# Recording VectorE and ScalarE in program order, with attention and norms placed by a clock at emission

## The chip, the cores and the metric

One core of a Trainium2 chip. The metric is device time in microseconds (us) of one execution; lower is better. Executions of one kernel in one set of runs lie within about 0.25% of each other (the kernel before beside the experiments, 27 runs: 1635.41 to 1638.25 us). The profiled span of a kernel is 1 to 2 us shorter than its timed median.

## The reference

Two rounds of a local attention layer and a gated feed-forward, each with a residual, on 2048 tokens of width 1024 in bf16 (F = 3584, 32 heads, window of 8 keys at distance 2):

```python
x = x + attention(layernorm(x), wqkv, wo)    # q.k over 8 keys, softmax, weighted sum of v, then @ wo
x = x + (silu(n @ w1) * (n @ w3)) @ w2       # n = layernorm(x)
# the same two lines once more, with the same weights
```

## The kernel before

Tokens go in 4 chunks of 512. Matmuls leave their sums in banks of 512 columns; copying a bank out, so that TensorE can use it again, is called evacuation here. A chunk passes the QKV projection (`ps`), attention in two halves of 256 tokens (on VectorE: products `pr` and `tm`, each summed by a tree of adds), the output projection (`po`, called an o-tile, one for 128 tokens), a layer norm, and the feed-forward (gate `pg`, up `pu`, down `acc`). q, k and v travel through DRAM to change their layout. TensorE stands in program order; the other engines are ordered by a scheduler with priorities.

```python
    ctx.enter_context(tc.manual_schedule(engines={mybir.EngineType.PE}))
    ...
    def tree_sum8(buf, dst):
        nc.vector.tensor_tensor(buf[:, 0:4, :], buf[:, 0:4, :], buf[:, 4:8, :], op=ALU.add)
        nc.vector.tensor_tensor(buf[:, 0:2, :], buf[:, 0:2, :], buf[:, 2:4, :], op=ALU.add)
        nc.vector.tensor_tensor(dst, buf[:, 0, :], buf[:, 1, :], op=ALU.add)
    ...
    for c in range(NCH):                       # the first layer's QKV, and attention of chunk 0
        for which in range(3):
            q_part(0, c, which)
            ...                                # cut: load x of later chunks
            if which == 1 and c == 1:
                nc.sync.dma_start(wo[:], wo_v)
            ...                                # cut: norm of the next chunk, o_tile(0, 0)
            if c == 3 and which == 1:
                o_tile(0, 1)
                ln_half(("B", 0, 0), 0, 0)     # norm for the first feed-forward
                o_tile(0, 2)
                o_tile(0, 3)
                ln_half(("B", 0, 0), 0, 1)
    ...                                        # cut
    # in the feed-forward, per 128 columns of F: 8 matmuls pg, 8 matmuls pu, then
                    with hp():                 # priority over attention
                        sg = sgp.tile([P, CH], BF16, name="sg")
                        nc.scalar.activation(sg[:], pg[:], ACTF.Silu)
                        nc.vector.tensor_tensor(hT[:, g0 + fi - f0, :], sg[:], pu[:], op=ALU.mult)
```

## Time and profile before

| | before |
|---|---|
| time, median of 4 runs | 1636.94 us (1636.28 to 1638.18) |
| profiled span | 1635.4 us |
| 7424 matmuls of 512 columns at 0.2158 us | 1602.3 us |
| start of the first QKV matmul | 13.92 us |
| beyond 1602.3 us, from there to the last matmul's end | 15.50 us |
| last matmul's end to the span's end | 3.69 us |

The 0.2158 us is a start-to-start distance: 192 undisturbed matmuls take 41.44 us. (The mean of 380 ns in the profile is the latency of one matmul; matmuls overlap.) I found the 15.50 us by listing every pair of neighbouring matmul starts that lie further apart than that. The three terms of the table and the first matmul's start add up to the span: 13.92 + 1602.3 + 15.50 + 3.69 = 1635.4.

The page's busy line, of the kernel before:

```profile
PE 1616.1 (99%) x7472; PEld 800.2 (49%) x7472; DVE 1152.4 (70%) x1961; ACT 340.5 (21%) x530; POOL 1.9 (0%) x12
```

Groups of TensorE's instructions, of the kernel before; the last column is idle time ahead of the group and who ended it:

```profile
L305 PE MATMUL pg<-xnT,w1t 128*128 128x512 bf16 x1792 | 424.7, 380 | 4.9 <-DMA xnT<-xn 4.9
...
L327 PE MATMUL acc<-w2t,hT 128*128 128x512 bf16 x1792 | 390.8, 379 | 5.1 <-DVE hT L314 4.7
L202 PE MATMUL ps<-xnT,wqkv 128*128 128x512 bf16 x1536 | 334.3, 380 | 1.8 <-ACT xnT L163 1.1 <-DVE x_sb L287 0.7
L283 PE MATMUL po<-wo,oT 128*128 128x512 bf16 x512 | 115.4, 379 | 0.0
```

TensorE is nearly full. What idles does so before the first feed-forward (waiting for its transposed norm), in the down projection (for the last product hT), and a little in QKV. The o-tiles wait for nothing.

TensorE's timeline at the first feed-forward, of the kernel before (start, duration, what, in brackets the idle time and its releaser):

```profile
187.09 8.85 PE L202 MATMUL ps<-xnT,wqkv 128*128 128x512 bf16 x40 [0.66 <-DVE x_sb L287]
200.80 3.28 PE L305 MATMUL pg<-xnT,w1t 128*128 128x512 bf16 x8 [4.86 <-DMA xnT<-xn]
203.87 2.23 PE L309 MATMUL pu<-xnT,w3t 128*128 128x512 bf16 x8
```

Eight matmuls normally take 1.89 us on this view; here 3.28, because after the 5 us of idling the next eight matmuls start 0.427 us apart instead of 0.216: half pace. And at the first down projection:

```profile
257.74 3.40 PE L327 MATMUL acc<-w2t,hT 128*128 128x512 bf16 x15
263.25 7.08 PE L327 MATMUL acc<-w2t,hT 128*128 128x512 bf16 x32 [2.11 <-DVE hT L314]
```

Fifteen matmuls use the first 15 slices of hT, the 16th waits for VectorE, where a 2.3 us transpose and a 1.2 us product of attention stood ahead of the last hT (259.03 to 262.51 us). VectorE sets this because it is full in the first third of the program. Windows of the kernel before, with busy time and, in brackets, number of instructions of each engine:

```profile
40.00:200.00 160.00, 155.28 (x719) 99.86 (x717) 149.88 (x263) 52.87 (x96) 0.00 (x0) 1.00 0.63 182
200.00:352.00 152.00, 147.23 (x673) 66.16 (x674) 150.48 (x251) 28.73 (x41) 0.00 (x0) 0.99 0.55 166
352.00:505.00 153.00, 152.25 (x707) 68.86 (x705) 151.98 (x262) 31.61 (x43) 0.00 (x0) 1.00 0.54 164
```

(third column: VectorE, 149.88 of 160, 150.48 of 152, 151.98 of 153 us). Where that begins is on VectorE's timeline:

```profile
53.04 0.17 DVE L129 RECIPROCAL rstd<-sd 128x2 f32<-128x2 f32 x1 [0.42 <-ACT sd L128]
56.59 2.36 DVE L228 TENSOR_TENSOR pr<-qT,kT 128x2048 bf16<-128x2048 bf16 x2 [3.38 <-DMA kT<-qkv_d_1_159]
```

Attention starts at 56.6 us, when its first keys (`kT`) land.

### The profile page before, as it was taken

To read this page: it belongs to the slowest core of one execution; us is meant where nothing else is said; L and a number is where in the kernel's file an instruction comes from. 1 tells how busy PE (TensorE), PEld (TensorE's weight loads), DVE (VectorE), ACT (ScalarE), POOL (GpSimd) and SP (SyncE) were. 2 spreads that over 40 slices of the span, in tenths; PEclk is the share of its full clock that TensorE was granted. 3 is DMA by queue.
4 is the path that set the end of the run, shared out by engine and by line. 5 is a ranking of instruction groups with operands and counts; after the bars stand their busy time and mean duration, and the time that the engine had idled before them with its cause. 6 is when DMAs were issued, how large, how long until landed. Compare 5 with 4: busy or idle time off the path is not lost.

```text
span 1635.4 us, 18944 instructions
## 1 busy us (share of the span) xinstructions
PE 1616.1 (99%) x7472; PEld 800.2 (49%) x7472; DVE 1152.4 (70%) x1961; ACT 340.5 (21%) x530; POOL 1.9 (0%) x12
## 2 busy tenths in 40 slices
PE   8999899999999999999999999999999999999999
PEld 5666444444444644446444554445544444444444
DVE  4899999999999781897728977299652992332212
ACT  3333311203021320223202232022320211121110
POOL 0000000000000000000000000000000000000000
PEclk9999999999999999999999999999999999999999
DMA  9943746557546774367743686438753574256440
GB/s 297 280 132 102 220 158 195 159 151 209 183 131 180 240 235 150 106 193 245 221 142 104 199 259 200 142 104 249 255 178 119 129 232 155 90 143 205 155 129 26
DMA packets 337113, 286.32 MB, mean 175 GB/s; under 512 B 69632, under 2 KB 319488, under 8 KB 336896
## 3 DMA queue, kind: packets, MB, share of 16 engines
q1 hardware_dynamic: 337024, 285.11, 57.2%
q8 instruction: 58, 0.95, 0.2%
q14 instruction: 31, 0.25, 0.0%
HBM read 239.99 MB, written 29.36 MB: 165 GB/s over the span
## 4 chain that ended last, share of the span: by engine, by line
PE 67%; DVE 29%; issue 3%; DMA 1%; ACT 0%; DVEq 0%; ACTq 0%
PE acc L327 21%; PE pg L305 15%; PE pu L309 15%; PE ps L202 13%; DVE pr L228 5%; DVE tm L273 4%; PE po L283 3%; DVE hT L314 3%; DVE tm L174 3%; DVE pr L174 2%; DVE x_sb L287 1%; DVE st L124 1%; DVE tm L175 1%; DVE pr L175 1%; DVE L L235 1%
## 5 line engine op out<-in xcount | busy, mean ns | idle before, releaser
L305 PE MATMUL pg<-xnT,w1t 128*128 128x512 bf16 x1792 | 424.7, 380 | 4.9 <-DMA xnT<-xn 4.9
L309 PE MATMUL pu<-xnT,w3t 128*128 128x512 bf16 x1792 | 423.7, 379 | 0.0
L327 PE MATMUL acc<-w2t,hT 128*128 128x512 bf16 x1792 | 390.8, 379 | 5.1 <-DVE hT L314 4.7
L202 PE MATMUL ps<-xnT,wqkv 128*128 128x512 bf16 x1536 | 334.3, 380 | 1.8 <-ACT xnT L163 1.1
L313 ACT ACTIVATE sg<-pg 128x512 bf16<-128x512 f32 x224 | 133.4, 597 | 843.2 <-PE pg L305 831.4
L314 DVE TENSOR_TENSOR hT<-sg,pu 128x512 bf16<-128x512 bf16 x224 | 152.1, 679 | 212.2 <-PE pu L309 210.7
L305 PEld LDWEIGHTS <-w1t 128*128 128x128 bf16 x1792 | 175.5, 98 | 217.0 <-issue 6.6
L327 PEld LDWEIGHTS <-hT 128*128 128x128 bf16 x1792 | 174.8, 98 | 218.5 <-DVE hT L314 9.0
L309 PEld LDWEIGHTS <-w3t 128*128 128x128 bf16 x1792 | 175.5, 98 | 212.0 <-issue 1.0
L202 PEld LDWEIGHTS <-wqkv 128*128 128x128 bf16 x1536 | 220.5, 144 | 114.6 <-issue 3.9
L332 DVE TENSOR_TENSOR x_sb<-x_sb,acc 128x512 bf16<-128x512 bf16 x128 | 87.0, 680 | 162.2 <-PE acc L327 162.2
L228 DVE TENSOR_TENSOR pr<-qT,kT 128x2048 bf16<-128x2048 bf16 x128 | 153.1, 1210 | 51.6 <-issue 32.1
L273 DVE TENSOR_TENSOR tm<-At,vT 128x2048 bf16<-128x2048 bf16 x128 | 151.7, 1213 | 0.3
L204 ACT CAST sgt<-ps 128x512 bf16<-128x512 f32 x192 | 108.7, 588 | 184.6 <-PE ps L202 151.7
L283 PE MATMUL po<-wo,oT 128*128 128x512 bf16 x512 | 115.4, 379 | 0.0
L124 DVE BATCH_NORM_STATS2 st<-x_sb 128x6 f32<-128x512 bf16 x120 | 79.9, 681 | 18.0 <-DMA x_sb<-in_A_x_dram 17.3
L174 DVE TENSOR_TENSOR pr<-pr 128x1024 bf16<-128x1024 bf16 x128 | 85.6, 680 | 0.0
L174 DVE TENSOR_TENSOR tm<-tm 128x1024 bf16<-128x1024 bf16 x128 | 84.4, 681 | 0.0
L283 PEld LDWEIGHTS <-oT 128*128 128x128 bf16 x512 | 50.0, 98 | 60.4
L287 DVE TENSOR_TENSOR x_sb<-x_sb,po 128x512 bf16<-128x512 bf16 x64 | 43.2, 677 | 15.4 <-PE po L283 15.4
L175 DVE TENSOR_TENSOR pr<-pr 128x512 bf16<-128x512 bf16 x128 | 51.8, 415 | 0.2
L175 DVE TENSOR_TENSOR tm<-tm 128x512 bf16<-128x512 bf16 x128 | 50.3, 415 | 0.1
(169 smaller groups left out, 428.7 us busy)
## 6 DMA issues: line engine op xcount, KB each, us to landing
w1t<-in_B_w_dram SPq DMA_DIRECT2D x56, 1024.0 KB, 5.4
w3t<-in_B_w_dram SPq DMA_DIRECT2D x56, 1024.0 KB, 7.2
w2t<-in_B_w_dram SPq DMA_DIRECT2D x48, 1024.0 KB, 5.4
wqkv<-in_A_wqkv_dram SPq DMA_DIRECT2D x28, 1024.0 KB, 6.6
w2t<-in_B_w_dram SPq DMA_DIRECT2D x16, 512.0 KB, 5.1
qkv_d_0_158<-sgt SPq DMA_DIRECT2D x16, 256.0 KB, 5.3
qkv_d_1_159<-sgt SPq DMA_DIRECT2D x16, 256.0 KB, 4.4
qT<-qkv_d_0_158 SPq DMA_DIRECT2D x8, 512.0 KB, 4.0
```

The costliest lines, as they stand in the source:

```text
L174: nc.vector.tensor_tensor(buf[:, 0:4, :], buf[:, 0:4, :], buf[:, 4:8, :], op=ALU.add)
L175: nc.vector.tensor_tensor(buf[:, 0:2, :], buf[:, 0:2, :], buf[:, 2:4, :], op=ALU.add)
L202: nc.tensor.matmul(ps[:], lhsT=ws[kk // KH][:, kk % KH, t::KT], rhs=xnT[:, kk, :], start=(kk == 0), stop=(kk == KT - 1))
L204: nc.scalar.copy(sgt[:, t - t0, :], ps[:])
L228: nc.vector.tensor_tensor(pr[:], qT[:], kT[:, :, k0:k0 + TCH], op=ALU.mult)
L273: nc.vector.tensor_tensor(tm[:], At[:], win, op=ALU.mult)
L283: nc.tensor.matmul(ps[:], lhsT=oT[:, t, j * P:(j + 1) * P], rhs=wo[:, t, hh * 512:(hh + 1) * 512], start=(t == 0), stop=(t == KT - 1))
L305: nc.tensor.matmul(pg[:], lhsT=w1t[:, kk, fi * P:(fi + 1) * P], rhs=xnT[:, kk, :], start=(kk == 0), stop=(kk == KT - 1))
L309: nc.tensor.matmul(pu[:], lhsT=w3t[:, kk, fi * P:(fi + 1) * P], rhs=xnT[:, kk, :], start=(kk == 0), stop=(kk == KT - 1))
L313: nc.scalar.activation(sg[:], pg[:], ACTF.Silu)
L314: nc.vector.tensor_tensor(hT[:, g0 + fi - f0, :], sg[:], pu[:], op=ALU.mult)
L327: nc.tensor.matmul(acc[:], lhsT=hT[:, f - f0, j * P:(j + 1) * P], rhs=w2ts[(f - f0) // 8][:, (f - f0) % 8, :], start=(f == f0), stop=(f == ...
```

## The change

VectorE and ScalarE also go into program order. Attention and norms become Python generators of single steps, each with a cost. While the program is emitted, a small clock keeps track of where TensorE, VectorE and ScalarE should be; before each evacuation of a bank it places as many attention steps as should end in time. O-tiles are emitted as soon as the clock says that their input is ready. The aim is that no evacuation stands behind a long attention instruction. The head is reworked too: x arrives on two queues, the fourth tile's statistics move to ScalarE, warm matmuls fill TensorE's gaps.

```diff
-    ctx.enter_context(tc.manual_schedule(engines={mybir.EngineType.PE}))
+    ctx.enter_context(tc.manual_schedule(engines={mybir.EngineType.PE, mybir.EngineType.DVE,
+                                                  mybir.EngineType.Activation}))
+    MM, TABLE, DMA = 0.216, 1.3, 2.5
+    x_at = [12.5] + [20.0 + 10 * c for c in range(1, NCH)]
+    def background(until):                      # norms first, then attention
+        while True:
+            for queue in (norms, attention):
+                s = head(queue)
+                if s is not None and max(now["dve"], s[1]) + s[0] <= until:
+                    take(queue)
+                    break
+            else:
+                return
 ... cut: the clock's counters, the norms as generators, the head
+    def tree(n, mul, dst):                      # attention's sums, interleaved
+        yield 1.14, 0.0, lambda: first(0)
+        for i in range(n):
+            yield 0.605, 0.0, lambda: half(i, 4)
+            if i:
+                yield 0.21, 0.0, lambda: half(i - 1, 1)
+            if i + 1 < n:
+                yield 1.14, 0.0, lambda: first(i + 1)
+            yield 0.34, 0.0, lambda: half(i, 2)
+        yield 0.27, 0.0, lambda: half(n - 1, 1)
 ... cut
+        qks[l, h] = qT, kT, max(now["dve"], qkv_at[l, h // R, 1]) + DMA     # keys "ready"
 ... cut
+            if c == NCH - 1 and which == 2:
+                between(False, True)            # force the o-tiles of chunk 0
             q_part(0, c, which)
 ... cut: the feed-forward
+                    r = max(pe(KT), ts)
+                    background(r + slack)       # slack -0.5 for the last two hT, else 1.0
+                    nc.vector.tensor_tensor(hT[:, f - f0, :], sg[:], pu[:], op=ALU.mult)
```

## The prediction

> **What bounds it.** TensorE: the page shows it busy 1616 of 1635.4 us at a granted clock of 0.998. There are 7424 matmuls of 512 columns; in undisturbed runs of the trace 192 of them take 41.44 us, 0.2158 us each, so they need 1602.3 us in any order. VectorE (70%) and ScalarE (21%) cannot set the total, but from 40 to 505 us VectorE is busy 94 to 99% (windows by stage), and there its order matters.
>
> **What can be won.** From the starts of consecutive matmuls, all beyond 1602.3 us:
> - 13.9 us before the first QKV matmul, then about 1.35 us lost at a slow pace (0.427 us apart). That is the unwarmed pace of the Trainium skill ("TensorE: Matmul & The Clock Gate", Part 1); this trace agrees.
> - 0.9 us at 187 us (QKV waits for a bank that VectorE frees late).
> - 5.0 us at 200.8 us: the first feed-forward waits for its normalised input, whose VectorE steps stood behind attention; then 1.6 us at the slow pace.
> - 2.3, 2.0 and 0.9 us at 263, 347 and 425 us, and five times 0.23: the down projection waits for the last hT, which stood behind a 2.2 us transpose or reduce.
> - 3.7 us from the last matmul's end to the span's end.
> The middle points make 15 us, 0.9%. After 510 us there are almost no gaps.
>
> **What the change does.** No matmul of the work goes; VectorE and ScalarE do the same arithmetic, now in program order. Attention is cut into steps of at most 2.3 us, placed only where the emission clock says they end before the next evacuation is due. The last two hT of a split get no slack, so the down projection's waits (6.4 us) should go. The first feed-forward's norm takes precedence over attention, and its last o-tiles stand 13.8 us of QKV ahead: 5.0 + 1.6 and 0.9 us should go. The head loads x on two queues, moves the fourth tile's statistics to ScalarE, splits evacuations and adds warm matmuls: first QKV matmul at 12.7 us, warm: 2 us won.
> The emission clock agrees with this trace's start-to-start times on VectorE (1.136 product, 0.602, 0.335, 0.202 tree; assumed 1.14, 0.605, 0.34, 0.21) and is generous for transposes (2.35 against 2.23), so VectorE should not drift late. Its DMAs are optimistic: 2.5 us against 4 to 8 us to landing. Attention's first keys landed at 56.6 us; from there two halves, norms and adds cost 116 us by these durations (estimate), against o-tiles that TensorE now reaches near 171 us. If keys land by 55 us it just holds; otherwise TensorE waits 1 to 4 us there.
>
> **Sum.** 12.7 + 1602.3 + 3.7 = 1618.7 us span, + 1.2 us between span and timed median = 1620; plus about 2 us of leftover or new waits: **1622 us**, 0.9% less. 8 in 10: 1618.5 to 1629. Over 2% faster (1603.8) lies below matmuls plus head: 0.01. Within 2%: 0.97. Slower: 0.02.
>
> **What would show it.** First QKV matmul near 12.7 us; no wait before the first feed-forward; waits of the down projection for hT under 1 us in all; VectorE's and ScalarE's busy times within 1%.
>
> **What would make it wrong.** The order is rigid: a late landing (keys, transposes) now holds every evacuation behind it, and o-tiles placed as soon as the clock says "ready" make TensorE wait directly for oT: new waits at po matmuls at 130 to 260 us. Or the warm matmuls delay the head's transposes and the head gains nothing.

## The result, and the profile after

| | before | changed |
|---|---|---|
| time, median of 4 runs each | 1636.94 us | 1634.37 us (1634.29 to 1634.40) |
| ratio | | 0.9983, 95% interval 0.9966 to 1.0001 |
| profiled span | 1635.4 | 1632.6 |
| first QKV matmul | 13.92 | 14.09 |
| beyond 1602.3 us until the last matmul's end | 15.50 | 12.44 |
| last matmul's end to the span's end | 3.69 | 3.73 |

Ratios, here and below, are the mean time of one kernel's runs over that of the other's of the same rounds, so not quite the ratio of the medians. The kernel before was run again beside each set of runs: medians 1636.94, 1637.14, 1637.32 and 1637.54 us, so medians of different sets can be compared to about 1 us. The interval of the changed kernel's ratio just includes 1: against the kernel before, nothing was gained beyond doubt.

The predicted 15 us did go, and almost as much came back elsewhere. Sums of the distances between matmul starts, beyond 0.216 us each:

| where, us | before | changed |
|---|---|---|
| slow pace just after the head | 1.4 | 0 |
| QKV matmuls waiting for a free bank | 0.9 | 2.2 (at 98 and 154) |
| o-tiles waiting for oT | 0 | 8.75 (177 to 186) |
| slow pace after these | 0 | 1.4 |
| first feed-forward waiting, and slow pace after it | 5.0 + 1.7 | 0 |
| down projection waiting for hT, 8 places | 6.4 | 0 |

From 189 us to the end the changed kernel's TensorE has no gap. Its busy line and the groups that answer to those of before:

```profile
PE 1614.9 (99%) x7479; PEld 801.0 (49%) x7479; DVE 1175.1 (72%) x1960; ACT 351.9 (22%) x542; POOL 1.9 (0%) x12
```

```profile
L535 PE MATMUL pg<-xnT,w1t 128*128 128x512 bf16 x1792 | 423.3, 379 | 0.0
...
L560 PE MATMUL acc<-w2t,hT 128*128 128x512 bf16 x1792 | 390.8, 379 | 0.0
L500 PE MATMUL ps<-xnT,wqkv 128*128 128x512 bf16 x1536 | 333.0, 379 | 2.3 <-ACT sgt L504 1.9 <-ACT xnT L275 0.5
L466 PE MATMUL po<-wo,oT 128*128 128x512 bf16 x512 | 118.7, 384 | 7.0 <-DVE oT L317 7.0
```

The idle time of `pg` and `acc` is gone; `po`, which waited for nothing before, waits for oT. (The profile counts 7.0 us from modelled ends; from start to start it is 8.75.) On TensorE's timeline of the changed kernel:

```profile
175.14 0.81 PE L466 MATMUL po<-wo,oT 128*128 128x512 bf16 x3
177.35 0.39 PE L466 MATMUL po<-wo,oT 128*128 128x512 bf16 x1 [1.41 <-DVE oT L317]
179.75 0.61 PE L466 MATMUL po<-wo,oT 128*128 128x512 bf16 x1 [2.01 <-DVE oT L317]
182.15 0.61 PE L466 MATMUL po<-wo,oT 128*128 128x512 bf16 x1 [1.79 <-DVE oT L317]
184.55 7.85 PE L466 MATMUL po<-wo,oT 128*128 128x512 bf16 x26 [1.79 <-DVE oT L317]
```

TensorE takes one slice of oT each 2.4 us, which is the time VectorE needs for one slice of attention: TensorE has caught up with VectorE and runs at its speed. In the kernel before, that half of attention ended at 160.4 us and TensorE reached its o-tiles at 174.2; here it ends at 185.1 and TensorE is there at 175.1. VectorE's timeline shows the last slices of that half, in the kernel before:

```profile
159.95 0.48 DVE L176 TENSOR_TENSOR oT<-tm 128x256 bf16<-128x256 bf16 x2
```

and in the changed kernel:

```profile
184.87 0.29 DVE L317 TENSOR_TENSOR oT<-tm 128x256 bf16<-128x256 bf16 x1
```

Why it ends 25 us later is on VectorE's timeline of the changed kernel, in three places:

```profile
47.95 0.17 DVE L202 RECIPROCAL rstd<-sd 128x2 f32<-128x2 f32 x1 [0.47 <-ACT sd L195]
60.08 1.23 DVE L370 TENSOR_TENSOR pr<-qT,kT 128x2048 bf16<-128x2048 bf16 x1 [11.96 <-DMA kT<-qkv_d_1_127]
...
70.72 0.29 DVE L317 TENSOR_TENSOR psm<-pr 128x256 bf16<-128x256 bf16 x1
71.04 1.23 DVE L370 TENSOR_TENSOR pr<-qT,kT 128x2048 bf16<-128x2048 bf16 x1
...
79.72 1.46 DVE L215 TENSOR_SCALAR xn<-x_sb,mv,rstd 128x1024 bf16<-128x1024 bf16 x3
83.70 0.55 DVE L215 TENSOR_SCALAR xn<-x_sb,mv,rstd 128x1024 bf16<-128x1024 bf16 x1 [2.53 <-DMA xnT<-xn]
```

First, the keys land at 60.1 us; the clock believed in about 44.6 (12.5 + 128 matmuls of 0.216, an evacuation, 1.25 and 2.5 us for the transfers). VectorE idles 12 us, with the statistics of a later chunk (6.7 us, done before the keys in the kernel before) standing behind the keys. Second, a tree's last add takes 0.32 us from its start to that of the next product (0.202 in the kernel before): that product overwrites the buffer that the add reads, and now stands directly behind it (that this is the reason was a guess here; the run pairs tests it). Third, four norm applies in a row need a fourth buffer of three and wait for a transpose. Also, half a norm and four residual adds, about 6 us, now stand ahead of the second half's values; in the kernel before they came later, and that was the 5 us wait of the feed-forward. Together, keys 3.5 us later than before, 6.7 of statistics, 3.3 of adds (28 of them), 5.1 of waits for transposes and 6.3 of norm and residual adds make about the 25 us.

Why the keys are late, on the DMA queue's timeline of the changed kernel:

```profile
44.07 0.57 SPq L597 DMA_DIRECT2D wo<-in_A_wo_dram  x1
44.74 0.40 SPq L506 DMA_DIRECT2D qkv_d_1_127<-sgt  x1
...
46.39 0.56 SPq L521 DMA_DIRECT2D w1t<-in_B_w_dram  x1
54.49 0.55 SPq L334 DMA_DIRECT2D kT<-qkv_d_1_127  x1
```

The 256 KB store of the last keys was issued 0.7 us behind the 2 MB load of wo, took 9.7 us, and the load of the keys had to wait for it. The trace has wo landing at 53.75 us and the store right behind it, at 54.43. In the kernel before, the store was issued at 45.27, ahead of wo (45.69), landed at 48.81, and the keys' load was issued at 48.87.

VectorE's lateness has a second consequence, on ScalarE, which now is in program order too:

```profile
83.96 1.28 ACT L390 ACT_TABLE_LOAD   x1
97.31 0.63 ACT L390 ACTIVATE E<-L 128x512 bf16<-128x512 f32 x1 [12.07 <-DVE L L389]
```

The exp was placed where the clock expected VectorE's logits. They came 12 us later, and all evacuations of QKV stood behind the exp, until TensorE ran out of banks:

```profile
98.47 1.89 PE L500 MATMUL ps<-xnT,wqkv 128*128 128x512 bf16 x8 [1.33 <-ACT sgt L504]
```

### The profile page after: what moved, and what is told of

The parts are those of the page before. It is cut to its first block, busy times and chain, and to the rows that moved or that the text cites. A ratio compares the mean times of both kernels' runs of the same rounds, so it can differ in the third digit from the quotient of the medians.

```text
span 1632.6 us, 18984 instructions
## 1 busy us (share of the span) xinstructions
PE 1614.9 (99%) x7479; PEld 801.0 (49%) x7479; DVE 1175.1 (72%) x1960; ACT 351.9 (22%) x542; POOL 1.9 (0%) x12
## 4 chain that ended last, share of the span: by engine, by line
PE 94%; DVE 5%; DMA 1%; ACT 0%; issue 0%; ACTq 0%; DVEq 0%
PE acc L560 24%; PE pu L543 24%; PE pg L535 24%; PE ps L500 16%; PE po L466 6%; DVE pr L370 1%; DVE tm L429 1%; DVE pr L315 1%; DVE tm L315 1%; DMA xnT<-xn 0%; DVE psmT L393 0%; DVE L L395 0%; DMA x_sb<-in_A_x_dram 0%; DVE psm L317 0%; DVE st_133 L244 0%
## 5 line engine op out<-in xcount | busy, mean ns | idle before, releaser
L370 DVE TENSOR_TENSOR pr<-qT,kT 128x2048 bf16<-128x2048 bf16 x128 | 156.5, 1222 | 75.5 <-DMA kT<-qkv_d_1_130 61.2
L429 DVE TENSOR_TENSOR tm<-At,vT 128x2048 bf16<-128x2048 bf16 x128 | 156.2, 1220 | 2.4
L315 DVE TENSOR_TENSOR pr<-pr 128x1024 bf16<-128x1024 bf16 (+1 forms) x256 | 134.4, 552 | 0.4
L315 DVE TENSOR_TENSOR tm<-tm 128x1024 bf16<-128x1024 bf16 (+1 forms) x256 | 133.4, 552 | 0.2
L466 PE MATMUL po<-wo,oT 128*128 128x512 bf16 x512 | 118.7, 384 | 7.0 <-DVE oT L317 7.0
L190 DVE BATCH_NORM_STATS2 st<-x_sb 128x6 f32<-128x512 bf16 x120 | 76.0, 671 | 0.3 <-DMA x_sb<-in_A_x_dram 0.3
L393 DVE STREAM_TRANSPOSE psmT<-psm 128x2048 bf16<-128x2048 bf16 x16 | 36.9, 2309 | 0.4
```

The lines of the kernel that those rows point to most:

```text
L315: nc.vector.tensor_tensor(b[:, 0:m, :], b[:, 0:m, :], b[:, m:2 * m, :], op=ALU.add)
L370: V.tensor_tensor(pr[:], qT[:], kT[:, :, k0:k0 + TCH], op=ALU.mult)
L429: V.tensor_tensor(tm[:], At[:], win, op=ALU.mult)
L466: nc.tensor.matmul(ps[:], lhsT=oT[:, t, j * P:(j + 1) * P], rhs=wo[:, t, hh * 512:(hh + 1) * 512], start=(t == 0), stop=(t == KT - 1))
```

## The experiments

The theory: the new waits come from the first chunk's attention on VectorE, which starts late (keys) and runs longer than assumed; the rigid order hands this lateness to TensorE at the o-tiles and through ScalarE. Rivals: the tree's new order alone (A); the norm applies in a row alone (B); the place of the o-tiles; and the clock's error as against the lateness itself. All runs were correct.

| run | time, us | ratio to before (95%) | first keys used | first QKV | beyond 1602.3 |
|---|---|---|---|---|---|
| changed kernel | 1634.37 | 0.9983 (0.9966 to 1.0001) | 60.1 | 14.09 | 12.44 |
| quiet | 1628.56 | 0.9948 (0.9934 to 0.9961) | 50.6 | 13.79 | 6.63 |
| pairs | 1631.81 | 0.9967 (0.9955 to 0.9980) | 59.6 | 13.77 | 9.81 |
| xnready | 1628.58 | 0.9949 (0.9937 to 0.9962) | 58.5 | 13.62 | 7.14 |
| xat | 1639.08 | 1.0012 (0.9999 to 1.0024) | 60.4 | 13.51 | 18.16 |
| clock | 1629.09 | 0.9953 (0.9941 to 0.9966) | 61.5 | 14.02 | 7.04 |
| late_o | 1635.26 | 0.9988 (0.9975 to 1.0002) | 59.3 | 13.85 | 13.90 |
| best | 1621.99 | 0.9907 (0.9894 to 0.9921) | 53.5 | 13.86 | 0.04 |
| best_xsync | 1621.35 | 0.9904 (0.9888 to 0.9919) | 54.5 | 12.95 | 0.04 |
| noquiet | 1627.22 | 0.9939 (0.9926 to 0.9951) | 62.7 | 13.12 | 7.26 |
| noclock | 1621.43 | 0.9903 (0.9890 to 0.9917) | 54.9 | 13.33 | 0.04 |
| minimal | 1628.83 | 0.9949 (0.9936 to 0.9961) | 55.0 | 12.95 | 8.33 |
| nowarm | 1623.29 | 0.9916 (0.9902 to 0.9929) | 55.8 | 13.63 | 1.16 |

The traces of quiet, pairs, xnready and xat hold only 7275 of the 7424 matmul records; the last column counts the missing ones in.

### quiet: three loads moved out of the way

```diff
-                nc.sync.dma_start(wo[:], wo_v)
+                nc.scalar.dma_start(wo[:], wo_v)      # ScalarE's queue is in program order
+            if c == 2 and which < 2:
+                first_w(which)                        # first w1t, w3t tile, also from ScalarE's queue
... cut: first_w, and the feed-forward taking these two tiles
```

> Same VectorE and TensorE order as the changed kernel; only the 2 MB load of wo and the first w1 and w3 tiles (1 MB each) leave the window 44 to 57 us: they are issued from ScalarE's queue in program order, at 84, 112 and 126 us. Theory (late keys start attention late, the rigid o-tiles pass this on to TensorE): the first keys land at about 51 us instead of 60.1, the waits at the o-tiles near 175 us fall from 8.9 to about 2 us, the waits for ScalarE at 98 and 154 us (2.2 us) vanish; about 1626.5 us, 8 less. Rival A (the attention tree's new interleaving slows VectorE) and rival B (four norm applies in a row wait for transposes): keys may come earlier but the time falls by under 3 us.

The keys came at 50.6 us and the waits at 98 and 154 us vanished. The DMA queue of quiet (compare with the fence above):

```profile
43.59 0.54 SPq L506 DMA_DIRECT2D qkv_d<-sgt  x1
46.18 0.55 SPq L334 DMA_DIRECT2D kT<-qkv_d  x1
```

The same store is done within 2.6 us instead of 9.7. The time fell by 5.8 us instead of 8: the waits at the o-tiles went from 8.75 to 5.4 us, not to 2. The chain from the keys to the end of the second half grew from 125.1 to 128.6 us, and VectorE's waits for norm transposes from 7.7 to 11.4 us. The three loads were moved together. The landings above point to wo: the store landed 0.7 us behind it, while w1t, issued after the store, landed only at 57.97 us, and w3t was issued (56.3 us) after the keys' load. wo alone was not moved.

### pairs: the old order of the tree

```diff
-        yield 1.14, 0.0, lambda: first(0)
-        for i in range(n): ...                        # the interleaved order above
+        for i in range(0, n, 2):
+            for k in (i, i + 1):
+                yield 1.14, 0.0, lambda: first(k)
+            for m, cost in ((4, 0.605), (2, 0.34), (1, 0.21)):
+                for k in (i, i + 1):
+                    yield cost, 0.0, lambda: half(k, m)
```

> The tree sums in the old order, two products at a time, with the same assumed costs; all else as in the changed kernel. In the changed kernel the last add of a tree takes 0.32 us start to start instead of 0.20, because the next product overwrites the buffer which that add reads. Rival A: busy VectorE falls from 1175 to about 1150 us and the time by about 3.3 us (28 adds of 0.117 us stand before the late o-tiles), to 1631; if the tree were the main cause, by 8. Late-keys theory: keys still land at 60 us, and at most those 3.3 us come back.

VectorE's timeline of pairs:

```profile
70.42 0.49 DVE L317 TENSOR_TENSOR psm<-pr 128x256 bf16<-128x256 bf16 x2
70.83 2.35 DVE L367 TENSOR_TENSOR pr<-qT,kT 128x2048 bf16<-128x2048 bf16 x2
```

Two last adds take 0.41 us from their start to the next product, 0.20 each again. The time fell by 2.6 us, close to the expected 3.3 (28 adds of 0.118 us). VectorE's busy time fell to 1160 us, not to 1150. So A is real and is a part, not the main cause.

### xnready: norm applies spread out

```diff
+            xn_free.append(now["dve"] + 4.5)          # when this apply's xn buffer is free again
... cut
-            yield 0.47, 0.0, lambda: apply(i)
+            yield 0.47, xn_free[-3], lambda: apply(i)
... cut: xn_free starts as three zeros
```

> The emission clock is told that a norm apply needs one of three xn buffers, free 4.5 us after the apply three before it, so that applies of four in a row are spread between attention steps. Rival B: the two waits of 2.5 us of VectorE for a transpose at 81 and 121 us vanish, the time falls by about 5 us to 1629. Late-keys theory: keys still at 60 us; what comes back is at most these 5 us.

As expected: waits for transposes 2.7 instead of 7.7 us, none of them between the keys and the end of the second half (5.1 before), and 5.8 us less time. The keys came at 58.5 us, 1.6 earlier than in the changed kernel though no transfer was moved, so up to 1.6 of the 5.8 may not be the edit's. B is real too, and about as large as the moved loads.

### xat: true arrival times of x

```diff
-    x_at = [12.5] + [20.0 + 10 * c for c in range(1, NCH)]
+    x_at = [12.5, 14.5, 32.0, 38.0]
```

> The emission clock gets arrival times of x near the real ones (14.5, 32, 38 us instead of 30, 40, 50), so that all statistics are emitted before attention's first product and fill the 12 us in which VectorE waits for keys. Expected: 6.7 us of statistics leave the chain behind the keys; keys land at 60 us as before; about 1628 us, 6 less. If the start of attention is not what the time hangs on, no change.

The sign is wrong: 4.7 us slower than the changed kernel. The statistics did move ahead of the keys, and the half of attention did end 6 us earlier (179.0). But a clock that is now right about x and still wrong about the keys runs further ahead of the chip. It placed the exp 10 us earlier in ScalarE's order. ScalarE of xat:

```profile
73.02 1.28 ACT L390 ACT_TABLE_LOAD   x1
91.00 0.63 ACT L390 ACTIVATE E<-L 128x512 bf16<-128x512 f32 x1 [16.70 <-DVE L L389]
```

and TensorE of xat:

```profile
92.15 2.29 PE L500 MATMUL ps<-xnT,wqkv 128*128 128x512 bf16 x5 [5.96 <-ACT sgt L504]
```

It also placed the second half's two o-tiles 10 and 7 us of matmuls earlier, where TensorE waited 8 us for them. The two errors of the old clock, pessimism about x and optimism about the keys, had partly cancelled.

### clock: the keys' true time, and nothing else

```diff
-        qks[l, h] = qT, kT, max(now["dve"], qkv_at[l, h // R, 1]) + DMA
+        qks[l, h] = qT, kT, max(now["dve"], qkv_at[l, h // R, 1]) + (18.0 if (l, h) == (0, 0) else DMA)
```

> Only the emission clock changes: it is told that the first keys are there at 60 us (the measured landing) instead of 44.6. No transfer, buffer or operation changes. Expected if the clock's error is what costs: the statistics of the last x chunk go ahead of the keys (6.7 us off the chain behind them), ScalarE's exp no longer stands ahead of evacuations it blocks (waits at 98 and 154 us, 2.2 us, gone), the waits at the o-tiles fall from 8.9 to 4 to 5 us; about 1628 us. If it is the late keys alone, with any order: no change, 1634.

5.3 us less, with the keys no earlier (61.5 us) and no transfer or operation changed. The waits of QKV behind an exp are gone; those at the o-tiles fell to 6.1 us: the statistics now stand ahead of the keys, and the chain from the keys to the end of the second half takes 118.7 us instead of 125.1. The order alone, given the late keys, is worth 5 us.

### late_o: the o-tiles forced later

```diff
-            if c == NCH - 1 and which == 2:
-                between(False, True)
             q_part(0, c, which)
+            if c == NCH - 1 and which == 2:
+                between(False, True)
```

> The two o-tiles of the second half are forced after the last QKV part instead of before it. If the cause were where the o-tiles stand, the 8.9 us of waits would go and the time fall by 5 us or more. If VectorE's chain behind the late keys is the cause, TensorE waits as long before the first feed-forward instead: 1632 to 1637 us.

1635.26 us. TensorE waits 5.1 us at the o-tiles and 2.8 us before the first feed-forward, and 3.8 us pass at the slow pace. The test was weaker than meant: without the force the clock itself put the o-tiles only 3.5 and 6.9 us of matmuls later, still inside the last QKV part. It shows that moving them a little trades one wait for another, not what a long move would do.

### best and best_xsync: all together

best is quiet + pairs + xnready + xat + the keys at 50.6 us in the clock (8.5 instead of 18.0). best_xsync also undoes the head's second queue:

```diff
-        (nc.scalar if j % 2 else nc.sync).dma_start(x_sb[:, j:j + 1, :], xin[:, j:j + 1, :])
+        nc.sync.dma_start(x_sb[:, j:j + 1, :], xin[:, j:j + 1, :])
```

> All together: wo and the first w1 and w3 off the window, old tree order, spread norm applies, arrival of x as measured, first keys at 50.6 us in the clock. The chain behind the keys is 10 us earlier and about 15 us shorter; no wait of TensorE over 0.5 us after the first QKV matmul; 13.7 + 1602.3 + 3.9 us of span, about 1622 us. If waits of over 3 us remain, something not yet named holds TensorE.

> As best, but the four x tiles are loaded on one queue, as in the kernel before. There the first tile was used at 3.8 us, in the changed kernel at 5.0. If the two queues delay the head, the first QKV matmul comes at about 12.9 instead of 13.7 us and the time is 0.8 us less than best; if the last tile counts, it is the same or later.

Both times are as expected; the way to them is not quite. The keys came at 53.5 us in best, not 50.6, and the chain behind them took 120.3 us: 5 less than in the changed kernel, where 15 was expected. xnready's spacing did not do its work here: VectorE still waits 6.6 us for transposes in this chain in best, and 5.9 us in best_xsync, at two places:

```profile
76.82 0.55 DVE L215 TENSOR_SCALAR xn<-x_sb,mv,rstd 128x1024 bf16<-128x1024 bf16 x1 [2.65 <-DMA xnT<-xn]
...
116.69 0.55 DVE L215 TENSOR_SCALAR xn<-x_sb,mv,rstd 128x1024 bf16<-128x1024 bf16 x1 [3.24 <-DMA xnT<-xn]
```

TensorE's busy line and its timeline in best_xsync:

```profile
PE 1612.6 (100%) x7479; PEld 801.0 (49%) x7479; DVE 1161.0 (72%) x1960; ACT 352.7 (22%) x542; POOL 1.9 (0%) x12
```

```profile
171.80 7.07 PE L465 MATMUL po<-wo,oT 128*128 128x512 bf16 x32
178.71 13.98 PE L499 MATMUL ps<-xnT,wqkv 128*128 128x512 bf16 x64
192.52 1.89 PE L544 MATMUL pg<-xnT,w1t 128*128 128x512 bf16 x8
```

No wait, no slow pace: 0.04 us beyond 1602.3 from the first QKV matmul to the last matmul. The o-tiles run through, and the first feed-forward starts at 192.5 us (206.1 in the changed kernel, 200.8 before). It is close: the second half's attention ends at 172.9 us, 1.1 us after TensorE began on its first slices and 0.4 us before it takes the last one (estimate: 7 matmuls of 0.216 us after 171.80).

In best_xsync the first x tile is used at 3.84 us, in best at 4.76, in the changed kernel at 4.99; the first QKV matmul follows at 12.95, 13.86 and 14.09. The Trainium skill ("DMA: Bandwidth & Descriptors", "Issuing engines are not separate DMA queues") says that transfers of different issuing engines "interleave with each other" on the same 16 DMA engines; this fits: two tiles at a time delay the first, and the head hangs on the first. The second queue cost where the change meant to gain: 0.9 us in the head of this pair, 0.6 us in its time. Over all runs the first QKV matmul came at 13.5 to 14.1 us with two queues (8 runs) and at 12.95 to 13.3 with one (4 runs with warm matmuls), 0.7 us apart on average.

### noquiet, noclock, minimal: what best_xsync needs

Each takes something away from best_xsync: noquiet leaves the three loads in the old place and tells the clock 60 us; noclock goes back to the old 2.5 us for the keys; minimal leaves out pairs and xnready.

> best_xsync without the change of transfers: wo, w1 and w3 load in the old window, and the clock is told the late landing of the keys (60 us). If late keys are a cause of their own and not only through the clock: keys near 60 us, the second half's attention ends about 6 us later than in best_xsync (172.9 us), TensorE waits 5 to 7 us at the o-tiles, 1626 to 1628 us. If a true clock and a lean chain suffice, 1621.5.

> best_xsync with the emission clock's old value for the first keys (2.5 us after the store, 44.6 us instead of 50.6). The order now has the second half's o-tiles 3.5 us of matmuls earlier. If a clock that runs ahead is what makes TensorE wait: 3 to 5 us of waits at the o-tiles or at evacuations behind an exp, 1624 to 1627 us. If the clock's error does not matter once the chain is short: 1621.5.

> best_xsync without the old tree order and without spread norm applies: are the two small costs of VectorE needed? The clock does not know of them, so it runs 6 to 8 us ahead by the second half's end, and its o-tiles stand 3.5 us earlier: waits of 5 to 9 us, 1626 to 1630 us. If they are slack by now: 1621.5.

noquiet: 1627.22 us, 7.26 us of waits and slow pace, as expected. With a true clock and a lean chain, late keys still cost 6 us. minimal: 1628.83 us, as expected: pairs and xnready together are needed, too. It ends the second half at 175.6 us, 2.6 later than best_xsync, and has its first o-tile 3.5 us of matmuls earlier. Which of the two edits does it was not separated; VectorE's waits for transposes in the chain (7.0 us, against 5.9 in best_xsync) hardly differ, so it isn't shown that xnready works by them here. noclock missed: no wait at all, 1621.43 us. So once the statistics stand ahead of the keys, a clock value 6 us further off (44.6 us, with the keys at 54.9) does no harm: this order ends the second half at 167.5 us, and TensorE comes for it at 168.7. It ends 5.4 us earlier than under best_xsync's better value largely because it happens to wait 0.7 us for transposes instead of 5.9. What counts is whether VectorE is there when TensorE comes, not whether the clock is exact. What clock alone gained had to do with this order of things, not with a correct number as such.

### nowarm: without warm matmuls in the head

```diff
-            warm(4)      # twice, and warm(2) once, between the head's transposes
```

> best_xsync without the ten warm matmuls between the head's transposes. If they keep TensorE at full pace: the first QKV matmul no later than 12.95 us, but 6 to 9 matmuls after it 0.427 us apart instead of 0.216, 1.3 to 1.9 us more, 1622.7 to 1623.3 us. If they only fill time: the same or 0.3 us less.

1.9 us more than best_xsync, as expected in sum but split otherwise: the first QKV matmul comes at 13.63 us, 0.7 later (the head with warm matmuls showed 12.95 to 13.33 in runs with one x queue, so up to half of this can be scatter), and 1.1 us are lost at the slow pace after it, none with them. For the pace the warm matmuls do what they are meant for; why the head itself came later stays open.

## Why the prediction was right or wrong

- Right: TensorE bounds the kernel, 1602.3 us of matmuls are a floor, and the old waits were sized and placed right. The down projection's 6.4 us, the first feed-forward's 5.0 + 1.7, the 0.9 at 187 us and the slow pace after the head are all 0 in the changed kernel.
- Right in mechanism: "a late landing (keys, transposes) now holds every evacuation behind it, and o-tiles placed as soon as the clock says 'ready' make TensorE wait directly for oT". The waits appeared at o-tiles, at 177 to 186 us.
- Wrong, the step that failed: "If keys land by 55 us it just holds; otherwise TensorE waits 1 to 4 us there", and with it "so VectorE should not drift late". Both terms of that sum were too small. The keys landed at 60.1 us, not by 55, because the scheduler's DMA queue put the 2 MB load of wo ahead of the last store of keys; the trace of the kernel before already said 56.6, and I had assumed better without a reason in the trace. The chain behind the keys took 125.1 us, not 116: 3.3 us from 28 tree adds whose cost I had read in the old order, and 5.1 from two waits of 2.5 us for norm transposes (the last 0.7 us were not traced). TensorE waited 8.75 us at the o-tiles, lost 1.4 at the slow pace after them and 2.2 behind a blocked exp, 12.4 us in all against the 2 allowed. quiet, pairs, xnready and clock each give back 2.6 to 5.8 us; best removes all of it, to 0.04 us. That it lands on the predicted 1622 us is partly luck: its first QKV matmul is 1.2 us later than predicted, and the 2 us allowed for leftovers are not there.
- Wrong: "first QKV matmul at 12.7 us". It came at 14.09, warm as predicted. Of the 1.4 us, 0.9 is the second x queue in the pair best and best_xsync, 0.7 on average over the runs; the rest was not traced.
- Together: predicted span 12.7 + 1602.3 + 2 + 3.7 = 1620.7 us; measured 14.09 + 1602.3 + 12.44 + 3.73 = 1632.6.
- Wrong: "VectorE's and ScalarE's busy times within 1%". VectorE rose by 2.0%, 22.7 us (15 of them the tree, by pairs; the rest was not traced), ScalarE by 3.3%, 11.4 us (9.0 from 66 table loads of 1.28 us instead of 59; the head's statistics also went to it).
- On the slow pace: the Trainium skill ("TensorE: Matmul & The Clock Gate", Part 1) puts the half-speed clock down to recent idling. The distances of 0.427 us after the 5.0 us wait of the kernel before, and after the row of waits at the changed kernel's o-tiles, agree; after its single waits of 2.3 and 2.0 us (263 and 347 us) the kernel before stayed at full pace.

Left open: whether moving wo alone would do as much as the three loads; why xnready's spacing fails in best; and whether o-tiles placed much later would have served.

## What to carry to other kernels

An order fixed at emission is as good as its worst assumption: a transfer time, a buffer that frees late or an add that waits for its neighbour is passed on to every engine that stands in order behind it, so compare each assumed ready time with the trace, above all of transfers. Correcting one wrong assumption of several can make things worse, because errors cancel; judge by whether the producer is there when the consumer comes. When an engine waits for a small transfer, look at what large transfers were issued just ahead of its store.

## What the Trainium skill lacked or had wrong

- "DMA: Bandwidth & Descriptors" ("Latency and other measured facts") has no figure for a small transfer behind a large one: a 256 KB store issued 0.7 us behind a 2 MB load took 9.7 us and landed 0.7 us after it; in quiet, where that load and the first weight tiles come later, it took 2.6 us.
- "VectorE: DVE Perf Modes" ("The DRAIN you can't avoid") has no figure for an instruction that overwrites what the one directly ahead of it reads: the next start came 0.32 us after that of a 256-column add, against 0.202 us where the next instruction touches another buffer.
- "TensorE: Matmul & The Clock Gate" (Part 1) speaks of an idle window of about 3.4 us before the clock drops; it gives no length for shorter idle times that add up. In the kernel before, TensorE's transposes ran at full pace (0.057 us apart, a quarter of the 0.216 us for a quarter of the columns) until 12.6 us and its matmuls at the slow pace from 13.92 us, after four idle times of 0.63 to 1.15 us between the transposes; in the changed kernel it was slow after waits of at most 2.2 us with single matmuls between them.
- "ScalarE: Activation LUTs" ("What ACT_TABLE_LOAD costs") agrees on the load (1.283 us), but the 1.38 us of draining that it adds for every switch, 2.66 us in total, was not seen: the instruction behind the 24 loads before a Silu, in the kernel before, started 1.29 us after the load's start (median), and where nothing else was waited for, 1.31 us passed from the end of the instruction ahead of the load to the start of the one behind.
